# One of nine rows per partition of an MLP weight block, loaded by two transfers over 124 and 4 partitions

## The chip, the core and the metric

The kernel runs on one core of a Trainium2 chip, the other cores idle. The metric is the time of one execution on the device in microseconds (us), as the median of several runs. A profile of one execution goes with it: the *span* runs from the first to the last recorded instruction of the core, and the time of the execution is a little longer than the span. The engines are named as the profile names them: PE (TensorE matmul), PEld (its weight loads), DVE (VectorE), ACT (ScalarE), POOL (GpSimd), SP (SyncE), and the sixteen DMA engines that move data between memory and the on-chip buffer.

## What is computed

A gated mix of an attention block over a window of a cache and an MLP, for one new token of each of eight sequences (`B = 8`, `D = 576`, `F = 4608`, 32 query heads, 16 key heads, head size 128, window 2048). All inputs are bf16.

```python
x = A_x                                             # [8, 1, 576]
g = sigmoid((x * gate_w).sum(-1, keepdims=True))
# A: attention over the last W = 2048 rows of the caches
q = (x @ wq)                                        # 32 heads of 128
p = softmax(q k^T * 128**-0.5)                      # k, v: [8, 16, 2048, 128] each
a = (p v) @ wo                                      # [4096, 576]
# B: MLP
h = gelu(layernorm(x) @ w1 + b1)                    # [8, 4608]
b = h @ w2 + b2                                     # w2: [4608, 576]
out = g * a + (1 - g) * b
```

Nearly all bytes are those of the two cache windows, 64 MiB each; `w2` has 5.3 MB.

## The kernel before

The kernel is a stream of large loads on SP's queue, with the arithmetic behind it. At the start SP loads `wq` and `w1`. Then 32 units of K and 32 of V of 2 MiB each come in turn, each into one of nine slots of the on-chip buffer (128 partitions x 16,384 B); after every eighth V unit follows a quarter of `wo`. A load waits until its slot has been read (`slot_free`). K units are transposed on DVE (L716) and multiplied on PE; V units are multiplied on PE (L751) and picked out of PSUM on DVE (L763, L764).

At the end of the stream stand the pieces that this change is about. `bias` (L816) loads `b2` as a broadcast over 6 and over 2 partitions. Then `m2_chunk` (L828) loads `w2` in four blocks of 1152 rows, `ci = 0` to `3`. A block lies in its slot as 128 partitions of nine rows of 576 elements (`FJ = 9`, one row is 1,152 B, nine are 10,368 B next to each other in memory and in the slot). Blocks 0 to 2 are one transfer each; block 3 is cut into four transfers of 4, 3, 1 and 1 rows per partition, so that PE can work on the first while the last arrive. Behind each transfer stands an `AccGroup` of matmuls (L608), two for each row, which add into one PSUM bank with the output projection of the attention. When all are done, DVE and ACT copy half of the bank each (L846, L847), and ACT issues the store.

What sets the order: every operation is given to a small planner with an engine, a cost, the operations that it waits for (`deps`) and operations that it must not be placed before (`after`). The planner puts the operations of each engine in an order by estimated start times (a load of 64 KiB or more is charged its bytes at 428 GB/s, one after another) and writes out the waits that are needed. All loads of SP are chained by `after`, so their order is the order of the stream: `K`, `V`, `W`, then `B` and `M` 0 to 3. Nothing on SP follows the `w2` loads except the final wait.

Two small loads at the start, on ACT's queue, have few partitions as well: `x` and the gate's weights over 8, 6 and 2 partitions, and `b1` over 4 partitions.

Of the kernel before, what the change touches and what calls it, by code (L numbers as in the profile page):

```python
# [38 lines left out]
class _Plan:  # L39
# [10 lines left out]
    def add(self, eng, fn, deps=(), name=None, cost=0.1, after=(), prio=0):  # L50
        op = _Op(eng, fn, deps, name, cost, after=after, prio=prio)
        op.idx = len(self.all)
        self.all.append(op)
        return op

    def dma(self, eng, fn, semkey, nbytes, deps=(), name=None, after=(), prio=0):
        op = _Op(eng, fn, deps, name, self.DMA_ISSUE, after=after, is_dma=True, dma_sem=semkey, nbytes=nbytes, prio=prio)
        op.idx = len(self.all)
        self.all.append(op)
        return op  # L60
# [146 lines left out]
def build_kernel(nc, A_x, A_k_cache, A_v_cache, A_wq, A_wo, B_x, B_w1, B_b1, B_w2, B_b2, gate_w, out):  # L207
    B, Sq, D = A_x.shape
# [12 lines left out]
    FC, FJ = 4, 9  # L221
# [11 lines left out]
    with ExitStack() as es:  # L233
# [80 lines left out]
        def view(name, parts=128):  # L314
            o, n, dt = R[name]
            a = arena[0:parts, o // 2: o // 2 + (n * (2 if dt == BF else 4)) // 2]
            if dt == F32:
                a = a.bitcast(F32)
            return a
# [19 lines left out]
        hT = view("hT").rearrange("p (t b) -> p t b", b=8)  # L339
# [23 lines left out]
        def slot(s):  # L363
            return RAW[:, s * SE:(s + 1) * SE]
# [24 lines left out]
        add, dma = P.add, P.dma  # L389
# [54 lines left out]
        for s in range(2):  # L444
            o_xz.append(add("dve", (lambda s=s: lambda e: e.tensor_copy(xz[:, s, :].rearrange("p (k z) -> p k z", z=2)[:, :, s], x_sb[:, 512:576]))(),  # L445
                            deps=dx + [o_xz0], name="xz%d" % s, cost=0.12))
# [12 lines left out]
        for s in range(2):  # L459
            o_yz.append(add("dve", (lambda s=s: lambda e: e.tensor_copy(yz[:, s, :].rearrange("p (k z) -> p k z", z=2)[:, :, s], y_bf[:, 512:576]))(),  # L460
                            deps=[o_y, o_yz0], name="yz%d" % s, cost=0.12))
# [30 lines left out]
        def b1ev_fn(e):  # L492
# [5 lines left out]
                   deps=[o_dga, o_dgb, o_onesf], name="g_pe", cost=0.4, after=[o_yTp])  # L498
# [7 lines left out]
        for q in range(4):  # L506
            o_i32.append(add("dve", (lambda q=q: lambda e: e.tensor_copy(i32[32 * q:32 * q + 32, :], ident[32 * q:32 * q + 32, 32 * q:32 * q + 32]))(),
                             deps=[o_ident, o_obl], name="i32_%d" % q, cost=0.15, prio=-1))
# [3 lines left out]
                   deps=o_i32, name="m4", cost=0.15, prio=-1)  # L512
        o_s8 = add("dve", lambda e: e.tensor_reduce(out=s8, in_=i32.rearrange("p (r n) -> p n r", r=4), axis=AXL.X, op=ALU.add),
                   deps=o_i32, name="s8", cost=0.15, prio=-1)
        o_mskt = add("dve", lambda e: e.tensor_reduce(out=mskt, in_=ident.rearrange("p (k t) -> p t k", t=WO_CH), axis=AXL.X, op=ALU.add),
                     deps=[o_ident, o_obl], name="mskt", cost=0.25, prio=-1)
# [70 lines left out]
        o_hT = add("dve", hs_fn, deps=[o_hf, o_gb], name="hT", cost=0.4)  # L587
# [44 lines left out]
        last_dma = [d_w1r]  # L632
        slot_free = [[o_qp]] * 3 + [[o_hp]] * 3 + [[]] * 3
# [15 lines left out]
        def take_slot():  # L649
            n = n_slot[0]  # L650
            n_slot[0] += 1
            return (n + 6) % NSLOT
# [158 lines left out]
        o_m2 = []  # L811
# [9 lines left out]
        def m2_chunk(ci):  # L821
            s = take_slot()
            dst = slot(s)[:, 0:FJ * D]
            src = B_w2[FCW * ci:FCW * ci + FCW, :].rearrange("(p j) n -> p (j n)", j=FJ)
            cuts = [0, 4, 7, 8, 9] if ci == FC - 1 else [0, FJ]
            ops = []
            for n, (j0, j1) in enumerate(zip(cuts, cuts[1:])):
                d = dma("sp", (lambda j0=j0, j1=j1: lambda e: e.dma_start(dst[:, j0 * D:j1 * D], src[:, j0 * D:j1 * D]))(),  # L828
                        ("t%d" % n) if ci == FC - 1 else ("s%d" % s), 128 * (j1 - j0) * D * 2, deps=slot_free[s] if n == 0 else [], name="d_w2_%d_%d" % (ci, n), after=last_dma[-1:])
                last_dma.append(d)  # L830
                mms = [(hT[:, FJ * ci + j, :], dst[:, j * D:(j + 1) * D]) for j in range(j0, j1)]
                ops.append(AccGroup("m2_%d_%d" % (ci, n), mms, [o_hT, d], cost=0.25 * (j1 - j0), after=o_m2[-1:]).op)
                o_m2.append(ops[-1])
            slot_free[s] = ops

        pv_hist = []
        for kind, i in stream:
            {"K": k_unit, "V": v_unit, "W": wo_chunk, "M": m2_chunk, "B": bias, "S": sums}[kind](i)
# [81 lines left out]
```

## Time and profile before

| | |
|---|---|
| time, median of 3 runs | 368.67 us (368.64 to 368.99) |
| time of the profiled execution | 368.67 us |
| its span | 366.5 us |
| busy: PE, DVE, ACT, POOL | 241.5, 248.4, 29.9, 42.3 us |
| bytes moved by DMA | 154.55 MB, mean 422 GB/s |
| queue of SP (q1) | 11,392 packets, 154.29 MB |
| packets under 2 KB | 1,588 |

The page gives, for each engine, the busy time and its share of the span, and then the span in 40 slices with a digit for the busy tenths of each. The DMA row is a mean over the sixteen DMA engines, so it cannot tell a slice in which all are nearly idle from one in which some have stopped and others have not; narrow windows at the end of the span can, since four busy engines of sixteen show as a share of 0.25. A packet is one row of a transfer (the bytes next to each other in one partition) or a write of four bytes that reports a finished share. The queue table separates what SP (q1) and ACT (q10) load from the fetches of instructions (q8 and q14), which run on the same sixteen DMA engines.

### The profile page before, as it was taken

What the parts mean: (1) busy time and instruction counts of PE and PEld (TensorE: products, weight loads), DVE (VectorE), ACT (ScalarE), POOL (GpSimd) and SP (SyncE); (2) the same over time, 40 slices, a digit from 0 to 9 for tenths busy, and PEclk for the clock granted to TensorE, in tenths of its full rate; (3) what the DMA queues carried; (4) which work ended last, traced back from release to release, by engine and by line L of the source; (5) the groups of instructions that cost most, each with busy time, mean ns of one, the idle gap of its engine ahead of it and who ended that gap; (6) DMA issues with size and microseconds to landing.
All of it is one profiled execution on the core that took longest, in us unless ns stands there. A gap on an engine that the chain in (4) does not pass through costs nothing.

```text
span 366.5 us, 3698 instructions
## 1 busy us (share of the span) xinstructions
PE 241.5 (66%) x1643; PEld 66.6 (18%) x1235; DVE 248.4 (68%) x384; ACT 29.9 (8%) x90; POOL 42.3 (12%) x166
## 2 busy tenths in 40 slices
PE   0349992986576359763786379682886379682575
PEld 0339100111011021101211021111111021111232
DVE  0804799699897767658796686659786776658410
ACT  1010002000300200003000300003000300003000
POOL 8030010011012000100011000100011000000000
PEclk9999998799699958968698858968698859967858
DMA  8999999999999999999999999999999999999994
GB/s 346 430 411 427 427 433 430 429 430 431 435 431 431 423 430 431 436 432 429 433 431 433 419 433 433 433 431 431 433 430 431 423 432 433 433 431 430 420 430 194
DMA packets 11465, 154.55 MB, mean 422 GB/s; under 512 B 1300, under 2 KB 1588, under 8 KB 2104
## 3 DMA queue, kind: packets, MB, share of 16 engines
q1 hardware_dynamic: 11392, 154.29, 98.7%
q8 instruction: 11, 0.18, 0.2%
q10 hardware_dynamic: 56, 0.04, 0.1%
q14 instruction: 6, 0.05, 0.0%
HBM read 154.31 MB, written 0.01 MB: 421 GB/s over the span
## 4 chain that ended last, share of the span: by engine, by line
DMA 47%; DVE 25%; PE 21%; SPq 3%; issue 2%; ACT 2%; POOL 0%
DMA arena<-in_A_v_cache_dram 34%; DVE arena L716 15%; DMA arena<-in_B_w_dram 14%; PE ps L392 9%; PE ps L751 4%; PE ps L397 3%; DVE arena L764 3%; PE ps L563 2%; SPq L828 2%; DVE arena L657 2%; DVE arena L676 1%; ACT arena L671 1%; DVE arena L763 1%; PE ps L608 1%; PE ps L685 1%
## 5 line engine op out<-in xcount | busy, mean ns | idle before, releaser
L716 DVE STREAM_TRANSPOSE arena<-arena 128x2048 f32<-128x2048 f32 x64 | 144.8, 2292 | 25.5 <-PE ps L392 13.0
L392 PE MATMUL ps<-arena 128*128 128x512 bf16 x408 | 134.3, 443 | 0.0
L397 PE MATMUL ps<-arena 128*128 128x512 bf16 x136 | 61.8, 454 | 38.6 <-DVE arena L716 28.1
L751 PE MATMUL ps<-arena 128*32 128x512 bf16 x512 | 39.1, 436 | 33.8 <-DMA arena<-in_A_v_cache_dram 33.8
L709 POOL COPY arena<-arena 32x32 bf16<-32x32 bf16 x128 | 26.0, 203 | 168.6 <-PE ps L392 155.9
L397 PEld LDWEIGHTS ps<-arena 128*128 128x128 bf16 x136 | 15.3, 112 | 143.4 <-issue 68.3
L657 DVE TENSOR_REDUCE arena<-ps 128x1 f32<-128x2048 f32 x8 | 18.3, 2282 | 21.0 <-PE ps L392 21.0
L764 DVE COPY_PREDICATED arena<-arena,ps 128x128 f32<-128x128 int32 x96 | 28.5, 300 | 3.0
L671 ACT ACTIVATE arena<-ps,arena 128x512 bf16<-128x512 f32 x32 | 21.6, 686 | 104.4 <-DVE arena L666 104.4
L769 PE MATMUL ps<-arena 128*128 128x8 f32 x64 | 13.9, 291 | 22.8 <-DVE arena L764 22.8
L763 DVE COPY arena<-ps 128x128 f32<-128x128 f32 x32 | 9.1, 284 | 27.4 <-PE ps L751 27.2
L751 PEld LDWEIGHTS ps<-arena 128*32 128x32 bf16 x512 | 11.8, 103 | 69.9 <-DMA arena<-in_A_v_cache_dram 36.4
L786 POOL TENSOR_TENSOR arena<-arena 128x128 bf16<-128x128 f32 x16 | 8.1, 508 | 135.3 <-ACT arena L778 135.3
L676 DVE STREAM_TRANSPOSE arena<-arena 128x512 bf16<-128x512 bf16 x32 | 21.5, 706 | 1.1 <-ACT arena L671 1.1
L769 PEld LDWEIGHTS ps<-arena 128*128 128x128 f32 x64 | 13.0, 238 | 42.0 <-DVE arena L764 39.7
L778 ACT ACTIVATE arena<-ps 128x16 f32<-128x16 f32 x16 | 2.9, 184 | 178.5 <-PE ps L769 178.5
L608 PE MATMUL ps<-arena 128*8 128x288 bf16 (+1 forms) x140 | 12.5, 333 | 1.9 <-DMA arena<-in_B_w_dram 1.4
L563 PE MATMUL ps<-arena 128*128 128x8 bf16 x144 | 9.8, 201 | 5.3 <-DMA arena<-in_B_w_dram 5.3
L563 PEld LDWEIGHTS ps<-arena 128*128 128x128 bf16 x144 | 9.7, 160 | 5.7 <-DMA arena<-in_B_w_dram 5.7
L472 PE MATMUL ps<-arena 8*128 8x8 bf16 x8 | 0.6, 174 | 13.0 <-DVE arena L445 9.4
L846 DVE CAST arena<-ps 8x288 bf16<-8x288 f32 x1 | 0.4, 444 | 12.4 <-PE ps L608 12.4
L686 DVE RECIPROCAL arena<-ps 128x32 f32<-128x32 f32 x8 | 2.8, 348 | 8.8 <-PE ps L685 8.8
(90 smaller groups left out, 89.0 us busy)
## 6 DMA issues: line engine op xcount, KB each, us to landing
arena<-in_A_k_cache_dram SPq DMA_DIRECT2D x32, 2048.0 KB, 34.9
arena<-in_A_v_cache_dram SPq DMA_DIRECT2D x32, 2048.0 KB, 34.5
arena<-in_B_w_dram SPq DMA_DIRECT2D x1, 4608.0 KB, 24.2
arena<-in_A_wo_dram SPq DMA_DIRECT2D x4, 1152.0 KB, 32.8
arena<-in_A_wq_dram SPq DMA_DIRECT2D x1, 4096.0 KB, 12.9
arena<-in_B_w_dram SPq DMA_DIRECT2D x3, 1296.0 KB, 33.3
arena<-in_B_w_dram SPq DMA_DIRECT2D x2, 576.0 KB, 28.6
arena<-in_A_wq_dram SPq DMA_DIRECT2D x1, 512.0 KB, 3.5
```

Of the source, the lines that this page charges most:

```text
L392: return e.add_instruction(mybir.InstMatmult(name=nc.get_next_instruction_name(), ins=[e.lower_ap(rhs), e.lower_ap(lhsT)], outs=[e.lower_a ...
L397: mm = e.matmul(outs[0], lhsT, rhss[0], start=start, stop=stop)
L563: ins = e.matmul(ps[:, BK_H, tt * 8: tt * 8 + 8], lhsT, yT[:, kt, :], start=(tt + kt == 0), stop=False, skip_group_check=True)
L608: ins = e.matmul(ps[32 * j:32 * j + 8, BK_ACC, 0:JN], lhsT, rhs[:, JN * j:JN * j + JN], start=False, stop=True, skip_group_check=True, til ...
L657: mx = add("dve", lambda e: e.tensor_reduce(out=k(MX), in_=ps[:, 0:4, :].rearrange("p a n -> p (a n)"), axis=AXL.X, op=ALU.max), deps=[qk_ ...
L671: return e.activation(out=Pm[:, 512 * c:512 * c + 512], in_=ps[:, c, :], func=ACTF.Exp, bias=k(NB), scale=SCALE, accum_out=k(SUM + c))
L676: pts.append(add("dve", (lambda c=c: lambda e: e.transpose(bass.AP(arena, offset=aoffs("PT") + (g % 2) * 2048 + 128 * c, ap=[[AST, 128], [ ...
L709: return e.tensor_copy(dst, src)
L716: tr = add("dve", (lambda h=h, kb=kb: lambda e: e.transpose(bass.AP(arena_f, offset=foffs("KT") + kb * 2048, ap=[[AST // 2, 128], [1, 2048]]),
L751: mm = e.matmul(ps[32 * t:32 * t + 32, BK_OS[i % 2], :], PT[:, g % 2, q, 32 * r4:32 * r4 + 32], slot(s)[:, 512 * r4:512 * r4 + 512], start ...
L764: return e.copy_predicated(dst, bass.AP(arena_i, offset=foffs("m4") + r, ap=[[AST // 2, 128], [0, 128]]), src)
L769: return e.matmul(ps[:, BK_S, 128 + 8 * (i % 2):136 + 8 * (i % 2)], osb[:, i % 2, :], s8, start=True, stop=True, skip_group_check=True)
```

## The change

For block 0 (`ci == 0`) the ninth row of each partition no longer travels with the other eight. Two transfers are issued for it ahead of the block's main transfer: one for partitions 0 to 123 and one for partitions 124 to 127, each on four engines. They take the wait for the slot; the main transfer then moves eight rows (9,216 B) of each of the 128 partitions. All three report on the semaphore of the slot, and the one group of matmuls of block 0 waits for all three and computes all nine rows as before. The bytes moved are the same. For the planner the two side transfers count 65,536 B more than they have, each.

```diff
             cuts = [0, 4, 7, 8, 9] if ci == FC - 1 else [0, FJ]
-            ops = []
+            ops, dside = [], []
+            if ci == 0:
+                cuts = [0, FJ - 1]
+                for n, (p0, p1) in enumerate(((0, 124), (124, 128))):
+                    j0 = cuts[-1]
+                    d = dma("sp", (lambda p0=p0, p1=p1, j0=j0: lambda e: e.dma_start(dst[p0:p1, j0 * D:FJ * D], src[p0:p1, j0 * D:FJ * D]))(),
+                            "s%d" % s, 65536 + (p1 - p0) * (FJ - j0) * D * 2, deps=slot_free[s] if n == 0 else [], name="d_w2s_%d" % n, after=last_dma[-1:])
+                    last_dma.append(d)
+                    dside.append(d)
             for n, (j0, j1) in enumerate(zip(cuts, cuts[1:])):
                 d = dma("sp", ...)
                 last_dma.append(d)
-                mms = [(hT[:, FJ * ci + j, :], dst[:, j * D:(j + 1) * D]) for j in range(j0, j1)]
-                ops.append(AccGroup("m2_%d_%d" % (ci, n), mms, [o_hT, d], cost=0.25 * (j1 - j0), after=o_m2[-1:]).op)
+                mms = [(hT[:, FJ * ci + j, :], dst[:, j * D:(j + 1) * D]) for j in range(j0, FJ if dside else j1)]
+                ops.append(AccGroup("m2_%d_%d" % (ci, n), mms, [o_hT, d] + dside, cost=0.25 * (j1 - j0), after=o_m2[-1:]).op)
                 o_m2.append(ops[-1])
             slot_free[s] = ops
```

## The prediction

> **What bounds the kernel now.** I read the page first: the busy line, the DMA lines, the queue table and the chain.
>
> ```profile
> span 366.5 us, 3698 instructions
> ...
> DMA  8999999999999999999999999999999999999994
> ...
> q1 hardware_dynamic: 11392, 154.29, 98.7%
> q8 instruction: 11, 0.18, 0.2%
> ...
> q14 instruction: 6, 0.05, 0.0%
> ```
>
> The sixteen DMA engines are busy in every slice except the first and the last, and SP's queue q1 alone takes 98.7% of their time. No compute engine comes near that. So the time is bytes over bandwidth, plus the head, plus what follows the last byte. The profiled execution took 368.67 us, 2.2 us around its span of 366.5, and the median of the runs is 368.67 too, so a difference in the span can be added to the median as it is.
>
> An average over sixteen engines hides one thing, and this change is about that thing: whether all sixteen stop together. So next I read the end of the chain of waits, and then the windows of the last microseconds (columns: span, five engines with instruction counts, PE clock, DMA share, GB/s).
>
> ```profile
> 339.20 24.71 DMA arena<-in_B_w_dram
> 363.96 0.31 PE ps L608 x2
> 364.26 0.02 issue
> 364.29 0.44 DVE arena L846
> ```
>
> ```profile
> 354.00:356.00 2.00, 1.69 (x17) 0.91 (x18) 0.00 (x0) 0.22 (x1) 0.00 (x0) 0.50 1.01 430
> ...
> 360.50:360.75 0.25, 0.00 (x0) 0.00 (x0) 0.00 (x0) 0.00 (x0) 0.00 (x0) 1.00 0.97 378
> ...
> 361.25:361.50 0.25, 0.25 (x8) 0.18 (x4) 0.00 (x0) 0.00 (x0) 0.00 (x0) 1.00 0.54 203
> ...
> 362.50:362.75 0.25, 0.25 (x6) 0.00 (x0) 0.00 (x0) 0.00 (x0) 0.00 (x0) 1.00 0.26 97
> 362.75:363.00 0.25, 0.06 (x2) 0.00 (x0) 0.00 (x0) 0.00 (x0) 0.00 (x0) 1.00 0.25 88
> 363.00:363.25 0.25, 0.03 (x2) 0.03 (x4) 0.00 (x0) 0.00 (x0) 0.00 (x0) 1.00 0.25 88
> 363.25:363.50 0.25, 0.25 (x6) 0.15 (x6) 0.00 (x0) 0.00 (x0) 0.00 (x0) 1.00 0.12 42
> 363.50:363.75 0.25, 0.25 (x8) 0.09 (x2) 0.00 (x0) 0.00 (x0) 0.00 (x0) 1.00 0.01 5
> ```
>
> The chain ends in the last piece of the second MLP matrix (L828), two matmuls (0.31), the copy out (L846) and the store. The windows show that the engines stop raggedly. At 360.75 all are busy, at 361.4 about half (0.54), from 362.5 to 363.25 a quarter, which is four of sixteen, then two, and from 363.5 next to none. The spread is some 3 us. A transfer is complete only when its slowest engine has delivered, so **the end is set by the last of these four engines, not by the mean**. Load added to a late engine costs its full time; load added to an early one costs nothing until the slack of up to 2.5 us is used.
>
> **The change part by part.** Block 0 has nine rows of 1,152 B per partition in one transfer over 128 partitions. After the change the ninth row travels in two transfers ahead of it, over 124 and over 4 partitions, each on four engines; the first eight rows follow as before.
>
> *What it takes off all sixteen.* Each engine carries 128/16 = 8 partitions. The 354-356 row gives 430 GB/s at share 1.01, which is 430/16.16 = 26.6 GB/s for one engine in rows of 10,368 B. Eight times 1,152 B less is 9,216 B, or 0.35 us less on each engine.
>
> *What it adds to four.* 124/4 = 31 rows, and 4/4 = 1, so 32 short rows on each of four engines. Their price is read where only the four late engines run and move the short last pieces: 97, 88 and 88 GB/s over four engines are 24.3 and 22 GB/s, so 1,152 B take 47 to 52 ns. 32 rows are 1.5 to 1.7 us, and I take 1.6, the middle. Net: **four engines +1.25 us (1.15 to 1.35), twelve engines -0.35 us**. The bytes are the same; only the division is worse.
>
> [...]
>
> *Which engines.* This decides the sign, and no view lists engines. The packet records behind the views have start, duration and size, and on one engine each packet begins as the one before it ends, so I followed sixteen chains through the run. Every engine has the same load but for the small transfers over 8, 6, 4 and 2 partitions and for the 17 instruction fetches of the rows q8 and q14 above. Each fetch falls on one engine and holds it back for about a microsecond, and nothing gives that back, because the queues never run dry. Engines with two or more fetches behind them, or with one very late, are the four that end last. The load of b1 over 4 partitions marks four engines near the start, and the two loads of b2 mark six near the end. By these marks one of the late four, the one that took three of the six 8 KB fetches, is among the four marked by b1, so among those that the change loads. The other three late ones are outside. Two chains ran in step for a while early on and could have been exchanged there, so this identification is likely and not sure. That engine stops in the window 363.25-363.50, say at 363.4, and the last one at about 363.55.
>
> *The sum.* That engine goes from 363.4 to 363.4 + 1.25 = 364.65; the other three late engines go back by 0.35 to at most 363.2. The last arrival moves from 363.55 to 364.65, **+1.1 us**. The two matmuls, the copy and the store behind it stay as they are. With the late engine of the four anywhere from 362.9 to 363.55 and the price from 1.15 to 1.35, the move is +0.5 to +1.35.
>
> *Issue and queue order.* SP issues two more transfers between the b2 loads and the first piece of L828. This is SP's record there, and how long a transfer lay in the queue:
>
> ```profile
> 318.63 0.36 SPq L828 DMA_DIRECT2D arena<-in_B_w_dram  x1
> ...
> 332.97 6.19 SPq L828 DMA_DIRECT2D arena<-in_B_w_dram  x1
> ...
> arena<-in_B_w_dram SPq DMA_DIRECT2D x3, 1296.0 KB, 33.3
> ...
> arena<-in_B_w_dram SPq DMA_DIRECT2D x2, 144.0 KB, 27.6
> ```
>
> An issue costs 0.36 us and the data lands some 28 to 33 us later, so two more issues (0.7 us) lie far under the backlog. One thing could hurt: the 6.19 us issue is SP held back by a queue that is full, and 31 rows on one engine take as many places as nearly four of the usual transfers of eight rows. Then the issues of the other pieces come later, by the time in which the four engines drain some 32 places: at the 0.6 us of a 16 KB row, about 19 us. Against 28 to 33 us of backlog that leaves about 10 us, so I cost it at nothing; without that cover, each microsecond of starvation would be a microsecond of time. SP has nothing but these loads behind it, and ACT, POOL and DVE issue nothing here, so no other queue waits.
>
> *The added wait.* The matmuls of block 0 now wait for the two side transfers as well as the main one. On PE these rows follow:
>
> ```profile
> 354.34 5.49 PE L608 MATMUL ps<-arena 128*8 128x288 bf16 x52 [0.31 <-ACT arena L805]
> 360.78 2.03 PE L608 MATMUL ps<-arena 128*8 128x288 bf16 x26 [0.96 <-DMA arena<-in_B_w_dram]
> ```
>
> The 52 are 16 of the output projection and 18 each of blocks 0 and 1. Block 0 will be complete on the late engine at most 1.25 us later than now. PE may stall there for up to a microsecond, with block 1 queued behind, but it has 0.96 us of idle time before the next wait and waits for later blocks on that same engine anyway. Cost nothing; if that cover were gone, at most 1 us. The planner counts 131,072 B more, 0.31 us of its own bandwidth figure, only for transfers at the end of the stream, which leaves the order before them alone.
>
> **The rivals.** *A, the forecast: a late engine is among the four.* +1.1 us, 369.8.
>
> *B, not slower: the four loaded engines all have slack.* If the chains were exchanged, the four stop at about 361.4 (where the share is 0.54) and go to 362.65, still ahead of the others, and the late ones outside go back by 0.35. The time is 368.67 - 0.35 = 368.3, a shade faster and below what can be measured. It turns at a slack of 1.25 us: with less the time rises, and from 1.6 up the whole 0.35 is gained. For it speaks that twelve of sixteen engines are early; against it, the marks above. [...]
>
> *C, worse: the deep side transfer starves the others.* If the full queue holds the main transfer of block 0 back past the moment when the early engines run out, each microsecond counts in full: 1 to 3 us on top, 370.5 to 372.5. For it speaks the 6.19 us issue, against it the 10 us left over.
>
> *D, the change does not do what it says*: if the side transfers spread over all sixteen engines, each carries 8 short rows, 8 x 50 ns = 0.40 us instead of 0.35, and the time stays at 368.7.
>
> **How the numbers follow.** A 0.80, B 0.11, C 0.05, D 0.04. A measurement of this kernel can tell about 0.2%, 0.74 us, from no change (the three runs span 0.35 us). A is beyond that in nine cases of ten, the rest being a late engine that stops early in its bound. Slower: 0.80 x 0.9 + 0.05 = 0.77. Same: 0.08 + 0.11 + 0.04 less 0.02 for the tails of B and D = 0.21. Faster: those 0.02. The predicted time is A's, 369.8. A's own range is 369.2 to 370.0; it reaches down to B at 368.3, which holds more than what lies above, and up to 370.3 for dearer short rows.
>
> **What would show it.** In the profile after, the last windows should show a share of about 0.06 to 0.25 (one to four engines) for over a microsecond longer than now, with the last arrival near 364.65 and PE's last two matmuls just behind; engines outside should stop about 0.35 earlier, so the share falls sooner. The total of bytes must be the same and the packets 128 rows more with 1,152 B. The prediction is wrong if the share falls to nothing by 363.2 (B), if there is a dip of the DMA share between 340 and 358 (C), or if the fetches fall on other engines than before, so that other engines come last.

## The result, and the profile after

The changed kernel takes 370.75 us (median of 6 runs, 370.52 to 371.59), the kernel before 368.65 us in the same runs. The ratio is 1.0059, with a 95% interval from 1.0046 to 1.0072. That is 2.1 us more, where 1.1 us was forecast, and above the top of the range (370.3). The profiled execution took 370.52 us with a span of 368.4, so the trace accounts for 1.9 us.

The tail is read first, in the same windows of the last microseconds as before (five engines, PE clock, DMA share, GB/s):

```profile
360.50:360.75 0.25, 0.25 (x6) 0.00 (x0) 0.00 (x0) 0.00 (x0) 0.00 (x0) 1.00 1.06 419
362.50:362.75 0.25, 0.13 (x4) 0.10 (x6) 0.00 (x0) 0.00 (x0) 0.00 (x0) 1.00 0.49 184
363.50:363.75 0.25, 0.25 (x8) 0.07 (x2) 0.00 (x0) 0.00 (x0) 0.00 (x0) 1.00 0.28 101
364.00:365.00 1.00, 0.65 (x8) 0.27 (x8) 0.00 (x0) 0.00 (x0) 0.00 (x0) 1.00 0.06 24
365.25:365.50 0.25, 0.25 (x8) 0.08 (x4) 0.00 (x0) 0.00 (x0) 0.00 (x0) 1.00 0.01 5
```

From 364.0 to 365.0 the share is 0.06, which is one engine of sixteen, moving 24 GB/s: one late engine alone, as forecast. But it stops at about 365.3 and not at 364.65. And the other engines do not stop 0.35 us earlier than before: the share is still 0.49 at 362.6, where it was 0.26. Something held back all sixteen. The rows for it stand a little further forward, where the side transfers run. Before, then after:

```profile
349.00:354.00 5.00, 3.31 (x30) 1.37 (x22) 1.19 (x4) 0.18 (x1) 0.51 (x1) 0.50 1.01 429
350.00:351.00 1.00, 0.57 (x8) 0.00 (x0) 0.35 (x2) 0.00 (x0) 0.00 (x0) 0.50 1.01 431
```

```profile
349.00:354.00 5.00, 3.27 (x30) 1.37 (x22) 1.19 (x4) 0.19 (x2) 0.51 (x1) 0.50 1.03 357
350.00:351.00 1.00, 0.50 (x8) 0.00 (x0) 0.42 (x2) 0.00 (x0) 0.00 (x0) 0.50 1.02 290
```

The DMA share is as full as before, so no engine waits for work, and yet 290 GB/s come out of it instead of 431. The packets take longer. Four engines on short rows cannot do that: at 22 to 24 GB/s each instead of 26.6 they would cost the sum 10 to 18 GB/s. Over the 5 us from 349 to 354, 72 GB/s are missing, 0.36 MB, which all sixteen move in 0.84 us. The packet records say the same. Of the 23 rows of 9,216 B that start between 349.8 and 350.6, none takes under 514 ns and one takes 561; before the change each takes 347. That is more rows than four engines could move in this time, so engines that have no part in the side transfers are slowed as well.

The end of the chain of waits and PE's last groups show that nothing else came in between (L854 is the copy that was L846):

```profile
348.75 17.01 DMA arena<-in_B_w_dram
365.75 0.04 issue
365.80 0.31 PE ps L608 x2
366.11 0.02 issue
366.13 0.45 DVE arena L854
```

```profile
359.54 1.27 PE L608 MATMUL ps<-arena 128*8 128x288 bf16 x18 [1.00 <-DMA arena<-in_B_w_dram]
362.62 2.03 PE L608 MATMUL ps<-arena 128*8 128x288 bf16 x26 [1.81 <-DMA arena<-in_B_w_dram]
```

The last piece is still issued 17 us before it lands (24.7 before the change), so the backlog shrank by 8 us, less than the 19 us allowed for, and nothing starved. PE waits for data before each block and is never what the data waits for.

**The theory after the result (P).** The time has two terms. One is the imbalance of the prediction, some 1.1 to 1.2 us on an engine that is late anyway. The other is a slowing of all sixteen engines, about 0.8 us, while some of them write rows into partitions that other engines serve. How many engines a transfer has is counted by its four-byte reports. Before, the 1,300 packets under 512 B are sixteen for each of SP's 79 large loads and one a partition, 36 in all, for the small loads and the store; after, there are 1,308, four more for each side transfer. So in the usual division, 128 partitions over sixteen engines, an engine has eight partitions, which are called its own here. In the side transfer over 124 partitions each of four engines has 31 rows. Together the four have 32 partitions of their own, so at least 92 of the 124 rows go to partitions of others. Which partitions belong to which engine is in no trace: where an experiment below is to choose between own partitions and others', the choice was the author's assumption. The rivals were that short rows slow the memory for all (Q), that short rows do on few engines (R, S) or by their number (T), or that only the imbalance costs (I).

### The profile page after: what moved, and what is told of

Its sections match the earlier page's. It is cut to its first block, busy times and chain, and to the rows that moved or that the text cites. A ratio compares the mean times of both kernels' runs of the same rounds, so it can differ in the third digit from the quotient of the medians.

```text
span 368.4 us, 3680 instructions
## 1 busy us (share of the span) xinstructions
PE 236.4 (64%) x1623; PEld 66.8 (18%) x1235; DVE 248.6 (67%) x384; ACT 30.0 (8%) x90; POOL 42.6 (12%) x166
## 2 busy tenths in 40 slices
DMA packets 11601, 154.55 MB, mean 420 GB/s; under 512 B 1308, under 2 KB 1724, under 8 KB 2240
## 4 chain that ended last, share of the span: by engine, by line
DMA 45%; DVE 28%; PE 20%; issue 2%; SPq 2%; ACT 1%; POOL 0%
DMA arena<-in_A_v_cache_dram 34%; DVE arena L716 16%; DMA arena<-in_B_w_dram 11%; PE ps L392 8%; PE ps L751 4%; DVE arena L764 4%; PE ps L397 3%; DVE arena L657 2%; PE ps L563 2%; DVE arena L676 2%; DVE arena L763 1%; ACT arena L671 1%; PE ps L769 1%; PE ps L685 1%; SPq L836 1%
## 5 line engine op out<-in xcount | busy, mean ns | idle before, releaser
L392 PE MATMUL ps<-arena 128*128 128x512 bf16 x401 | 130.7, 435 | 11.8 <-DVE arena L716 5.1
L397 PE MATMUL ps<-arena 128*128 128x512 bf16 x123 | 54.6, 444 | 31.4 <-DVE arena L716 24.6
L751 PE MATMUL ps<-arena 128*32 128x512 bf16 x512 | 40.6, 449 | 35.2 <-DMA arena<-in_A_v_cache_dram 35.2
L854 DVE CAST arena<-ps 8x288 bf16<-8x288 f32 x1 | 0.4, 445 | 14.3 <-PE ps L608 14.3
```

The lines of the kernel that those rows point to most:

```text
L392: return e.add_instruction(mybir.InstMatmult(name=nc.get_next_instruction_name(), ins=[e.lower_ap(rhs), e.lower_ap(lhsT)], outs=[e.lower_a ...
L397: mm = e.matmul(outs[0], lhsT, rhss[0], start=start, stop=stop)
L751: mm = e.matmul(ps[32 * t:32 * t + 32, BK_OS[i % 2], :], PT[:, g % 2, q, 32 * r4:32 * r4 + 32], slot(s)[:, 512 * r4:512 * r4 + 512], start ...
```

## Experiments

All times are medians, with the kernel before timed in the same series.

**e1_one128: the ninth row in one transfer over 128 partitions.**

```diff
-                for n, (p0, p1) in enumerate(((0, 124), (124, 128))):
+                for n, (p0, p1) in enumerate(((0, 128),)):
```

> The ninth row of block 0 goes ahead in one transfer over 128 partitions, eight rows on each of sixteen engines. Theory P (two terms: 32 more rows on an engine that is late anyway, about 1.2 us, and a slowing of all sixteen engines while four of them write rows into partitions that other engines serve, about 0.8 us): neither term is here, so 368.7, rows of 9,216 B stay at 347 ns. Rival Q (short rows at a stride of 10,368 B slow the memory for everybody, however many engines read them): rows beside the side transfer grow and the time is 369.3 or more.

368.59 against 368.61 us, ratio 1.000 (0.9991 to 1.001). Row of the windows:

```profile
350.00:351.00 1.00, 0.51 (x8) 0.00 (x0) 0.40 (x2) 0.00 (x0) 0.00 (x0) 0.50 1.00 422
```

The same bytes in the same short rows at the same stride cost nothing when all sixteen engines carry them in the usual division. Q falls. Nor is it an extra transfer, the order ahead of the main transfer or the added wait of the matmuls.

**e2_three: three engines instead of four.**

```diff
-                for n, (p0, p1) in enumerate(((0, 124), (124, 128))):
+                for n, (p0, p1) in enumerate(((0, 123), (123, 128))):
```

> Side transfers over 123 partitions (three engines, 41 rows each) and 5 partitions (five engines, one row each). By the imbalance term of theory P it matters which engines carry the rows: if the late engine of the four is the fourth, it is now spared and loses a row's time of eight partitions, the three others have slack for 41 rows (2.0 us), and only the slowing of all is left: 369.0 to 369.3. If the late engine is the third, 371.2. Rival S (no imbalance, the whole 2.1 us is the slowing by long runs of short rows on few engines): three engines for longer, 370.5 to 371.

369.26 against 368.61 us, ratio 1.0016 (1.0006 to 1.0025).

```profile
349.00:354.00 5.00, 3.30 (x30) 1.35 (x22) 1.19 (x4) 0.18 (x1) 0.51 (x1) 0.50 1.03 365
350.00:351.00 1.00, 0.53 (x8) 0.00 (x0) 0.39 (x2) 0.00 (x0) 0.00 (x0) 0.50 1.00 285
```

By the author's count three engines carry 41 rows each, ten more than in the change, and the slowing is nearly the same (365 GB/s, 0.75 us missing), but the time rises by 0.65 us instead of 2.1. With one engine fewer the imbalance is gone. If the three are among the four of the change, the late engine is the one they leave out, which is called the fourth here; S falls. What is left is the slowing, less the 0.35 us that the late engines now carry less: 0.75 - 0.35 = 0.4 us. The measured 0.65 us leave some 0.2 us unexplained.

**e4_own and e5_foreign: the same extra load, into two sets of partitions.** Both are the kernel before with six more transfers, into unused room of block 0's slot; the data is not used. In e5_foreign 64 is added to every partition of e4_own. The author took the first set for the four engines' own and the second for others'.

```diff
+            if ci == 0:
+                for n, p0 in enumerate((0, 1, 2, 3, 32, 33)):          # e5: (64, 65, 66, 67, 96, 97)
+                    d = dma("sp", (lambda p0=p0: lambda e: e.dma_start(
+                        bass.AP(arena, offset=p0 * AST + aoffs("RAW") + s * SE + FJ * D, ap=[[4 * AST, 4], [600, 5], [1, D]]),
+                        src[p0 % 4:p0 % 4 + 16:4, 0:5 * D].rearrange("p (j n) -> p j n", j=5)))(), ...)
+                    last_dma.append(d)
```

> The kernel before with six extra transfers ahead of block 0, each five rows of 1,152 B on each of four engines (30 rows an engine), into unused room of the slot; the data is not used. [...] Theory P: the late engine gets 1.45 us, nothing else slows, rows of 10,368 B stay at 389 ns: 370.1. Rival R (short rows on few engines slow all, wherever they land): 370.9, the same as with partitions from 64 on.

> [...] Theory P: the same 1.45 us on the late engine and a slowing of all beside it, some 0.8 us: 370.9, rows of other engines up to 500 ns and more during about 1.5 us. Rival R: the same time as with the partitions from 0 on.

e4_own took 369.77 us and e5_foreign 373.09 us, against 368.61: ratios 1.0035 (1.0022 to 1.0048) and 1.0118 (1.0101 to 1.0135). First e4_own, with a row of its tail, then e5_foreign, with a row of its tail and the last matmuls of PE:

```profile
349.00:354.00 5.00, 3.06 (x28) 1.19 (x18) 1.19 (x4) 0.40 (x2) 0.50 (x1) 0.50 1.02 428
350.00:351.00 1.00, 0.28 (x4) 0.00 (x0) 0.59 (x3) 0.00 (x0) 0.00 (x0) 0.50 1.05 444
364.00:364.50 0.50, 0.16 (x4) 0.12 (x6) 0.00 (x0) 0.00 (x0) 0.00 (x0) 1.00 0.06 23
```

```profile
349.00:354.00 5.00, 3.21 (x30) 1.35 (x22) 1.19 (x4) 0.18 (x1) 0.51 (x1) 0.50 1.02 305
350.00:351.00 1.00, 0.47 (x8) 0.00 (x0) 0.45 (x2) 0.00 (x0) 0.00 (x0) 0.50 0.91 196
367.00:368.00 1.00, 1.00 (x12) 0.55 (x10) 0.00 (x0) 0.00 (x0) 0.00 (x0) 0.50 0.01 3
364.42 4.48 PE L608 MATMUL ps<-arena 128*8 128x288 bf16 x36 [0.76 <-DMA arena<-in_B_w_dram]
```

This pair separates the terms. The bytes, the rows, the number of transfers and the number of engines are the same (154.69 MB and 1,324 packets under 512 B in both, 24 more than before: four reports for each of the six); only 64 is added to each partition. With the partitions from 0 on the rate holds (428 and 444 GB/s), one engine alone works on at the end (0.06 at 364.25), and the time rises by 1.16 us: **this is the imbalance by itself**. With those from 64 on the rate falls to 196 GB/s and the time rises by 4.5 us. R falls.

P is confirmed in kind, in so far as the partitions alone decide; that they do so by whose they are is not shown. Its size for e5_foreign was off (370.9 expected). The 4.5 us are not all slowing of the sixteen engines: 124 GB/s missing for 5 us are 1.44 us. Two more things are in the trace. By the packet records, the last twenty short rows follow one another on one engine and take 103 ns on average instead of 51, which holds that engine back by another 1.0 us. And the last load is over soon after 367 (share 0.01), but PE is at work until 368.9: its last 36 matmuls run at a granted clock of 0.50 and take 4.48 us, where in the kernel before the clock at the end is 1.00. Before, PE ended 0.7 us after the last engine; here it ends 1.7 us after it, another 1.0 us. With the 1.16 us of the imbalance these make 4.6 us, close to the 4.7 us between the two spans (371.2 and 366.5). Why the clock stays low is not shown; PE stood idle longer ahead of it, busy for 0.42 us between 356 and 358 where it was busy for 2.00 before.

Why the slowing is larger here than in the change (196 against 290 GB/s between 350 and 351) is not shown.

**e10_own3: the partitions of e4_own, on three engines.** As e4_own, with three partitions in each transfer, so that by the author's count three engines carry thirty rows more. P, with over 2 us of slack for these three and nothing slowed, put the time at 368.5 to 368.8.

```diff
-                        bass.AP(arena, ..., ap=[[4 * AST, 4], [600, 5], [1, D]]),
+                        bass.AP(arena, ..., ap=[[4 * AST, 3], [600, 5], [1, D]]),
```

> [...] Rival U (more rows on any engine show in the time): 369.5 to 369.8, as with four engines.

368.66 against 368.60 us, ratio 1.000 (0.9991 to 1.001).

```profile
349.00:354.00 5.00, 3.32 (x30) 1.36 (x22) 1.19 (x4) 0.18 (x1) 0.50 (x1) 0.50 1.01 427
```

Thirty rows more on each of three engines cost nothing that can be measured (U falls). They are paid out of slack; with a fourth engine loaded as well (e4_own), the cost is 1.16 us. So it is not how much is loaded but on whom.

**e6_112 and e7_two: slowing without imbalance.** The partitions of the side transfers were cut at 112 (sixteen engines with seven rows, then one row) and at 62 and 126 (two engines with 31 rows, the rest spread). The packets under 512 B give the engines: 1,332 in e6_112, 32 more than before, sixteen for each side transfer, and 1,320 in e7_two, 2 + 16 + 2 more. That most rows of e6_112 go to other engines' partitions was assumed by the author.

```diff
+                for n, (p0, p1) in enumerate(((0, 112), (112, 128))):               # e6_112
+                for n, (p0, p1) in enumerate(((0, 62), (62, 126), (126, 128))):     # e7_two
```

> [...] Theory P (own partitions cost nothing, other engines' partitions slow all): no imbalance, some slowing, 368.9 to 369.3, and rows of 9,216 B beside it above 347 ns. Rival I (only the imbalance between engines costs): 368.6.

> Side transfers over 62, 64 and 2 partitions: two engines get 31 + 4 + 1 rows, the other fourteen 4. The two engines have over 2 us of slack in the profile before, so no imbalance is left, and each of the other engines even carries four rows less (0.17 us). Theory P: only the slowing by two engines writing elsewhere, perhaps two thirds of that with three: 368.9 to 369.2. Rival I: 368.4.

e6_112 took 369.33 and e7_two 369.15 us against 368.58: ratios 1.0021 (1.0012 to 1.0031) and 1.0015 (1.0005 to 1.0025). First e6_112, then e7_two:

```profile
349.00:354.00 5.00, 3.23 (x30) 1.33 (x22) 1.19 (x4) 0.23 (x2) 0.50 (x1) 0.50 1.02 383
```

```profile
349.00:354.00 5.00, 3.32 (x30) 1.36 (x22) 1.19 (x4) 0.18 (x1) 0.50 (x1) 0.50 1.02 382
```

I falls: e6_112 gives every engine exactly the load of the kernel before, and still costs 0.75 us, with 46 GB/s missing for 5 us (0.54 us). Its missing bytes explain most of that, not all. e7_two has 47 GB/s missing, 0.55 us, less some 0.17 us for four rows fewer on the late engines; it too took about 0.2 us more than that.

**e8_near and e9_long: which partitions, and which rows.** Both start from e5_foreign.

```diff
-                for n, p0 in enumerate((64, 65, 66, 67, 96, 97)):
+                for n, p0 in enumerate((16, 17, 18, 19, 48, 49)):                   # e8_near
-                        bass.AP(arena, ..., ap=[[4 * AST, 4], [600, 5], [1, D]]),
+                        bass.AP(arena, ..., ap=[[4 * AST, 4], [D, 5], [1, D]]),     # e9_long
```

> [...] Theory P in the form that two engines writing to one group of partitions get in each other's way: as slow as from 64 on, 372.5 to 373.5. Rival H (the price is for crossing from one half of the partitions to the other): no slowing, 369.8 as with own partitions.

> As the six extra transfers with partitions from 64 on, but the five rows of a partition lie next to each other in the slot, so that they can go as one row of 5,760 B. The bytes and the partitions are the same. Theory P by bytes: the same slowing, 372.5 to 373.3. Rival T (it is the number of short rows that slows the others): clearly less, 370 to 371.

373.29 and 372.75 us against 368.58, ratios 1.0122 (1.0107 to 1.0137) and 1.0112 (1.0097 to 1.0127). First e8_near, then e9_long:

```profile
349.00:354.00 5.00, 3.14 (x30) 1.26 (x22) 1.19 (x4) 0.26 (x2) 0.50 (x1) 0.50 1.01 305
350.00:351.00 1.00, 0.37 (x4) 0.00 (x0) 0.54 (x2) 0.00 (x0) 0.00 (x0) 0.50 1.10 240
```

```profile
349.00:354.00 5.00, 3.34 (x30) 1.39 (x22) 1.19 (x4) 0.18 (x1) 0.50 (x1) 0.50 1.03 322
350.00:351.00 1.00, 0.57 (x8) 0.00 (x0) 0.34 (x2) 0.00 (x0) 0.00 (x0) 0.50 0.93 210
```

In these two runs, too, PE runs at 0.50 until 367 or later, so the rates compare better than the times. The partitions of e8_near, 16 to 31 and 48 to 61, are below 64 like those of e4_own, where the rate held at 428 GB/s, and they are as bad as those from 64 on (305 GB/s in both), so it is not a crossing of halves (H). Rows of 5,760 B, five times as long (the packet records show 24 of that size), are nearly as bad as short ones (322 GB/s), so it is not the number of rows (T).

**e11_twice: the change for two blocks.**

```diff
-            if ci == 0:
+            if ci <= 1:
```

> The change made twice, for block 0 and for block 1. Theory P: both terms are paid again, since nothing later gives the late engine its time back: about twice 2.1 us, 372.4 to 373.0. Rival V (the second is hidden behind what the first made late): 371 to 371.5.

372.88 against 368.60 us, ratio 1.0113 (1.0097 to 1.013). That is 4.3 us, twice the 2.1 of one block, and V falls. But the loads do not explain all of it. By the packet records the last engine stops at 367.0, 3.4 us later than before, and PE then works on until 368.5, again at half the clock:

```profile
364.26 4.28 PE L608 MATMUL ps<-arena 128*8 128x288 bf16 x36 [0.95 <-DMA arena<-in_B_w_dram]
```

With one block the last engine stopped 1.8 us later than before. So the two terms of the loads are paid nearly twice over, and that the time came out at just twice is partly luck: 0.9 us of it is PE.

## Why the prediction was wrong, point by point

- *What bounds the kernel*: right for the change. The sixteen DMA engines carry the time, and the last of them sets the end; e4_own and e10_own3 show it without anything else changed.
- *Which engines*: right in its result. One of the late four is among those that the change loads: from 364.0 to 365.0 one engine works alone, and it stops 1.8 us later than the last one before. The sum put all 32 rows on the same four engines and took them for those of b1. No view lists engines, so no run shows this directly. SP's record fits it: issuing the two side transfers took 14.34 us, 0.25 of them for the first, so the second, with four rows in all, was held back until part of the backlog had drained, and the main transfer behind it, with 128 rows, was not held back like that (its issue took 1.16 us). e2_three and e10_own3, with three engines, cost 0.65 and 0.06 us; by the author's count they leave out the fourth.
- *The price of the imbalance*: right in size. 1.1 us was summed; e4_own measures 1.16 us for 30 rows with nothing taken off, not far from what the same sum gives for it: 30 x 50 ns, less the 0.15 to 0.2 us that this engine is ahead of the last, or 1.3 to 1.35 us.
- *What it takes off all sixteen, 0.35 us, and the sum*: **this is the step that failed**. The sum let every other packet keep its length while the side transfers run. They do not: 0.84 us of all engines' work is lost between 349 and 354, and 1.1 + 0.84 = 1.94 us is close to the 1.9 us between the two profiles and the 2.1 us between the medians. What the side transfers do to the packets beside them was put at nothing, without a reason: the price of a short row was read from the last pieces of block 3, where every engine has its usual partitions, and carried over to a transfer that divides the partitions differently. The short rows themselves became only a little dearer (59 ns on average over the 136 of that time, against 51). It is the other engines' rows that grew. No bound was set for that, so the range ended at 370.3.
- *Issue order, the full queue, the added wait*: cost nothing, as worked out, though SP was held for those 14 us. The measured 370.75 lies in the range of rival C (370.5 to 372.5), but that is chance: C foresaw starvation, with a dip of the DMA share between 340 and 358. The rate fell there, while the share stayed at 1.0 (1.03 from 349 to 354). That pair of columns tells the two apart. Rivals B and D did not happen.

## What to carry to other kernels

Where the sixteen engines are full to the end, read the end of the DMA share in narrow windows: the time is that of the last engine. Here some 1.5 us of extra rows (30 at 50 ns) cost nothing that could be measured on three early engines (e10_own3, 0.06 us) and 1.16 us with a late one among four (e4_own). Keep large loads over all 128 partitions, not 124 and 4, nor 112 and 16: leaving the usual division cost 2.1 us in the change, and 0.75 us for the 147 KB of e6_112, where each engine carries the same bytes as before. Read the DMA share and the rate side by side. In the change a full share with a lower rate (1.02 and 290 GB/s) went with longer packets (514 to 561 ns instead of 347); at the end of the kernel before, a share and a rate that fall together (0.25 and 88 GB/s) were engines that had stopped. And before a difference between two times is put down to loads alone, check that the last engine still ends the kernel: in e5_foreign and e11_twice PE does, 1.7 and 1.5 us behind it.

## What the runs showed of the hardware

In these runs it depends on where the rows of a few engines land whether the whole core slows: between 350 and 351 it falls from 431 to 290 GB/s in the change, with at least 92 of 124 rows in partitions that other engines write in the usual division, and to 196 in e5_foreign, while e4_own, with 64 taken off each partition, holds 444. More engines are slowed than carry side rows (the 23 rows of 9,216 B in the change). They are not always slowed alike. From 352.7 to 355.1 in e5_foreign, with one chain of short rows left, 90 rows of 10,368 B start by the packet records: 86 of them take 389 to 451 ns, and four take 751 to 832. Three of these four follow one another, so one engine is slowed far more than the rest.

No run here shows where the rows are held up, and why engines without side rows are slowed too stays open.

Single instruction fetches seem to matter as well to the end of this kernel. In the kernel before, the packet records show a fetch of 16 KB that takes 948 ns at 357.9, and a row of 10,368 B that starts as it ends takes 880 ns instead of 389. There are seventeen fetches, 0.23 MB of 154, and the sixteen engines end 3 us apart. That the fetches are the cause of this spread is read from the packet records and was not tried by an experiment.
